# A weight fetched as eight long rows and turned by TensorE, with its cast moved from VectorE to ScalarE and GpSimd

## The chip, the cores and the metric

The kernel runs on one core of one Trainium2 chip. The metric is the device time of one execution in microseconds (us); the time before is the median of three runs, 203.02 us (202.86 to 203.06).

The names used below: PE is TensorE, DVE is VectorE, ACT is ScalarE, POOL is GpSimd, SP is SyncE. ACT and SP also issue DMAs (ACTq and SPq in the profile). A core has 16 DMA engines.

## The reference: what is computed

Two inputs `a` and `b` have the shape (8, 6400, 128), in float32. First a linear recurrence runs along the 6400 steps, for each of the 8 batches and 128 channels:

```python
h = a[:, t] * h + b[:, t]
out[:, t] = h
```

Its result, read as x with 51200 rows (tokens) of 128, goes through a mixture of eight small adapters. `logits = x @ w_gate` (w_gate is 128 x 8), the two largest logits of each token are taken, and a softmax over these two gives two weights. Each chosen expert e adds its weight times `(x @ A[e]) @ B[e]`, with A of shape (8, 128, 16) and B of shape (8, 16, 128). The result is x plus these two terms.

## The kernel before, in words

The 51200 tokens are cut into 100 chunks of 512 tokens. The chunks pass through these stages:

- SP loads `a` and `b` (line 295) into the tiles `a_tm` and `b_tm`, tokens on partitions: single chunks at both ends (256 KB for each of `a` and `b`), double chunks in the middle (512 KB).
- PE transposes both, by multiplying with an identity (line 310), so that channels are on partitions. ACT copies the turned `a` from PSUM to `a_st` (line 338); the turned `b` is read from PSUM.
- DVE runs the recurrence with a scan instruction, 512 steps at once, into `xT` in float16 (line 360).
- PE multiplies each block of 128 tokens with the 136 columns of `Awg_h` (line 434): 128 columns hold A for all experts, (e, r) in a row, and 8 hold the gate. ACT copies the result to `zl` (line 441).
- DVE, POOL and ACT make the gates of a group of chunks (lines 466 to 499), POOL or DVE multiplies them into `zl` (line 523), PE transposes the product (line 531), and ACT or DVE copies it (line 540).
- PE adds x and the product with `B_h` in PSUM (lines 558 and 559), ACT copies the sum to `outt` (line 566), and SP stores it (line 591).

The weights come at the start. Three DMAs on ACT's queue (line 261) fetch A, the gate and B into `cst_f`, in float32. A lies in memory as (e, d, r) and is wanted as d on partitions and (e, r) along them; the access pattern `moe_A.rearrange("e d r -> d e r")` does that in the DMA, in pieces of r = 16 floats, 64 bytes. One DVE cast (line 267) turns all 264 columns of `cst_f` into float16 in `cst_h`, of which `Awg_h` and `B_h` are parts. POOL makes the identity (lines 247 to 254), DVE casts it (line 263), and PE runs 14 transposes of the identity with itself (line 265), whose result is used by nothing, between the first real ones.

The order of the work is written out by hand. Each operation is added with its engine, a one-letter kind and the operations that it depends on; the strings in `ORDER` give the sequence of kinds on each engine, and within a kind the operations keep the order in which they were added. Each engine works strictly in its order. The wait of each operation is derived from its dependences (`waits`). PE's order begins with 11 transposes of kind "w" and then `ababwwwazb`: a and b of chunk 0, a and b of chunk 1, three more "w", a of chunk 2, the first logits matmuls "z" and b of chunk 2. ACT's order begins with the three weight DMAs, an activation that loads its table, three copies "a" and four copies "z". DVE's begins with the identity's cast, the weights' cast "c" and three scans. SP's order holds the loads x (of `a`) and y (of `b`) and the stores o. PSUM has eight banks; six of them rotate (`RING`) among the uses that name none, and each use waits until the bank's last content has been copied out.

A load waits until its slot of `a_tm` or `b_tm` has been transposed out (four slots of four blocks each for `a` and for `b`), an output copy until its part of `outt` has been stored (18 chunks fit).

Of the kernel before, what the change touches and what calls it, by code (L numbers as in the profile page):

```python
# [17 lines left out]
WARM = 14  # L18
# [3 lines left out]
RING = [0, 3, 4, 5, 6, 7]  # L22
ORDER = {
    "pe": (
        "wwwwwwwwwwwababwwwazbzzzaabzfzzffzzzfttffzdzdfzfzfzzzzfftfzzfddtffdzzzfdzzfzfztfzzfzztddfdfzfzdtfzzf"
        "dzzzzfttdffzddtfzzzfdddfzdzzffzttzzffzdtdzzffddzfztzffzzzddfdtffzzddfdztffzzzzdzftfztdfdzfddzdtzffzz"
        "dztzffdztdzdffzzzddtfztdzffdddztffzzdzzftdftzddzfdzfztzfzfddftzdzzfdtzzfzddtzzfddfftdzzfztfdzzztfddf"
        "fzzddtzdzfztfddfztzzffddfzztddtfzzzffdfzztdzddtffddztddfbtazddztzbzzbzzzadatdazbzzbdzztddtdztdddztdd"
        "dtddtddddttdd"
    ),  # L30
    "act": (
        "ccciaaazzzzaauzuazazazzzattaazzoozauazazzzzauatazzaootaauzzoaozzzaazztzaazztuzoaoaoazzoazzaozzzztaao"
        "auzooazzazoooazozazzaztuazzaozzoaaoozazztaazozzauootaazzoooazaazzzozzatzaauooazozooazzazzoazaouzzooa"
        "azzozouazoaazooozaazzzzotaaoozouzaozzatzzaoaoaozzzoazzazoouzazooaatozzzaauzozzoaoaaozzozzaotzaouozaz"
        "azaooazzootzazzuaaaozzzotooaauoozaooazoozzzzzzzaoauotauzzzozztoozouoozootooouuooooooo"
    ),
    "dve": (
        "icsss11223344s66ss1s2s31s2s43s64s6sss1s2s34s6ssss1s234ss6ssts1s23st4s6stss1s23s4sts6stss1s2s34ss1s62"
        "s3sts4s6s1s2t34s6stssts12st3s4ststs6sts1s234sts6ss1s234stssts612ts3s4sst6sstsst12346sssts1s234stss6s"
        "st12m34s6stststs1m2132436s4ss1m2m63m4t6mtm121m23m43m4t66tmmtt"  # L40
    ),
    "pool": (
        "cc8855pqpqrrmm585qp8rmmpqrmm85pqrmmmmm58mpqrmmmmmm58pqrmmmm8m5mpqrmmmm5m8mpqrmmmm8mm5qprm58mmmmmpqrm"
        "m58mmmpqrmmmmmm58pmqrm5mmmm8mqprmm5mm8qmprmmmm58mmmpqrmmmmm58mpqrmmm58mqmprmmm85mq8p5mrpq8r5pqr8558p"
        "pqqrr"
# [24 lines left out]
class Program:  # L70
# [8 lines left out]
    def add(self, eng, kind, deps, emit, sem=None, dur=0.0, lock=False, alt=None, size=0, ring=None):  # L79
        op = Op()  # L80
        op.i = len(self.ops)
        op.eng, op.kind, op.emit, op.sem = eng, kind, emit, sem
        op.deps = list({d.i: d for d in deps if d is not None}.values())
        op.cnt, op.clock, op.pos = 0, None, self.at
        op.dur, op.lock, op.alt, op.size = dur, lock or eng == "pool", alt, size
        op.ring = ring
        self.ops.append(op)
        return op
# [66 lines left out]
def bass_associative_scan_2x2__then__mixture_of_adapters_kernel(  # L155
# [9 lines left out]
    E = moe_w_gate.shape[1]  # L165
    R = moe_A.shape[2]
# [6 lines left out]
    of = out  # L173
# [16 lines left out]
    with ExitStack() as stack:  # L190
# [43 lines left out]
        eng = {}  # L234
# [19 lines left out]
        )  # L254
        o_c = []
        for key, dur, dst, src in (
            ("ca", 0.94, cst_f[:, 0:128].rearrange("p (e r) -> p e r", e=E), moe_A.rearrange("e d r -> d e r")),
# [9 lines left out]
        o_ch = P.add("dve", "c", o_c, lambda: eng["dve"].tensor_copy(cst_h[:, :], cst_f[:, :]), dur=0.3)  # L267
# [281 lines left out]
        def out_chunk(c, e_t):  # L549
# [15 lines left out]
            o_oe[c] = P.add("act", "o", [o_D[c]] + [out_user[p0 + k] for k in range(4)],  # L565
# [17 lines left out]
        def store(c, n):  # L583
# [5 lines left out]
            op = P.add(  # L589
                "sp", "o", [out_user[p0 + k] for k in range(nb)],  # L590
                lambda: eng["sp"].dma_start(
                    tokens(of, c, n, 4 * m), outt[:, p0 : p0 + nb, :].rearrange("p (h j) d -> p h (j d)", j=4 * m)),
                sem=dma_sem(f"st{p0 // 4}"), size=n if m > 1 else -n)
            for k in range(nb):
                out_user[p0 + k] = op
            o_st.append(op)
# [106 lines left out]
```

## Time and profile before

| | |
|---|---|
| median of three runs | 203.02 us (202.86 to 203.06) |
| the profiled execution | 202.82 us |
| its span, first to last instruction | 201.0 us |
| busy in the span: PE, DVE, ACT, POOL | 90%, 88%, 89%, 66% |
| HBM read and written | 52.56 MB and 26.21 MB, 392 GB/s over the span |

All numbers of the profile are from the one profiled execution. It was 0.2 us faster than the median, and 1.8 us of it lie outside the span. A row that begins with two times is a stretch of the span. "DMA share" is the time that the packets started in a stretch took, as a share of 16 engines' time: about 1 means full, and it can be a little over, since packets overlap. A row of DMA issues gives the tile and tensor, the queue, the count, the size of each and the median time from issue to the last byte's landing. In the chain of waits, a row is start, length and what was worked on. Rows of the timeline have start, length, engine, line, operation, tiles, shapes and the count of merged instructions, and in brackets the idle time before with what ended it.

### The profile page before, as it was taken

Reading aid. Unit: us, or ns where it says so; the run is one execution under the profiler, and the core shown is the slowest. Engines: PE = TensorE matmul, PEld = TensorE weight load, DVE = VectorE, ACT = ScalarE, POOL = GpSimd, SP = SyncE. Lnnn points to the kernel's source line nnn. Section 1 sums busy time; section 2 is a strip of 40 time slices with the busy share of each in tenths; the row PEclk is TensorE's granted clock in tenths of the full one; section 3 lists DMA queues with packets and bytes.
Section 4 is the critical chain, followed back from the end, with each engine's and each line's share of the span. In section 5 each row is a group of like instructions: output and inputs, shape, how many; then the busy total and the mean of one; then the engine's idle time right before and its main releaser. Section 6 shows DMA issues by size and latency. Waiting matters only on the chain.

```text
span 201.0 us, 7651 instructions
## 1 busy us (share of the span) xinstructions
PE 181.4 (90%) x3150; PEld 164.5 (82%) x3150; DVE 177.3 (88%) x265; ACT 178.4 (89%) x383; POOL 132.9 (66%) x209
## 2 busy tenths in 40 slices
PE   6878899899999996999999999999999998999840
PEld 6667678789989986999999999988888887998830
DVE  0799999999989996899999999998999999999830
ACT  3579899999999999699999999998899987999940
POOL 1061483959594954967898887697797978586400
PEclk9999999999999999799999999999999999999995
DMA  7999999999999999999999999999999999999992
GB/s 184 394 412 404 410 405 400 414 411 406 419 408 412 410 414 406 414 417 406 412 408 412 415 409 415 417 408 414 412 416 407 412 415 402 408 416 363 381 401 83
DMA packets 24690, 79.27 MB, mean 394 GB/s; under 512 B 3792, under 2 KB 3920, under 8 KB 24656
## 3 DMA queue, kind: packets, MB, share of 16 engines
q1 hardware_dynamic: 23328, 78.65, 98.0%
q8 instruction: 25, 0.41, 0.8%
q10 hardware_dynamic: 1328, 0.14, 0.5%
q14 instruction: 9, 0.07, 0.1%
HBM read 52.56 MB, written 26.21 MB: 392 GB/s over the span
## 4 chain that ended last, share of the span: by engine, by line
PE 36%; DMA 32%; ACT 17%; SPq 5%; DVE 4%; issue 2%; POOL 1%; ACTq 0%
DMA out_dram<-outt 16%; PE ps L310 14%; DMA a_tm<-in_a_dram 8%; DMA b_tm<-in_b_dram 7%; PE ps L558 6%; ACT outt L566 6%; PE ps L434 6%; SPq L295 5%; PE ps L559 5%; PE ps L531 5%; ACT zl L441 5%; ACT a_st L338 4%; DVE xT L360 2%; ACT zwT L540 2%; DVE zw L523 1%
## 5 line engine op out<-in xcount | busy, mean ns | idle before, releaser
L360 DVE TENSOR_TENSOR_SCAN xT<-a_st,xT,ps 128x512 f16<-128x512 f32 x96 | 120.3, 1253 | 7.6 <-PE ps L310 4.3
L523 POOL TENSOR_TENSOR zw<-zl,g 128x512 f16<-128x512 f32 x88 | 91.9, 1065 | 7.0 <-PE ps L531 5.4
L310 PE MATMUL ps<-ident_f,a_tm 64*128 64x64 f32 (+1 forms) x768 | 68.2, 231 | 6.5 <-DMA a_tm<-in_a_dram 2.7
L310 PE MATMUL ps<-ident_f,b_tm 64*128 64x64 f32 (+1 forms) x768 | 68.5, 231 | 1.2 <-DVE xT L360 1.0
L310 PEld LDWEIGHTS ps<-ident_f,a_tm 64*128 64x128 f32 (+1 forms) x768 | 56.2, 140 | 14.8 <-DMA a_tm<-in_a_dram 4.3
L338 ACT COPY a_st<-ps 128x512 f32<-128x512 f32 x100 | 61.5, 637 | 7.3 <-PE ps L310 7.0
L441 ACT COPY zl<-ps 128x408 f32<-128x408 f32 (+1 forms) x138 | 65.8, 540 | 0.9 <-PE ps L434 0.7
L566 ACT COPY outt<-ps 128x512 f32<-128x512 f32 x100 | 59.6, 640 | 3.7 <-PE ps L559 2.7
L558 PE MATMUL ps<-ident_h,xT 128*128 128x128 f16 x400 | 57.3, 232 | 0.7 <-issue 0.3
L310 PEld LDWEIGHTS ps<-ident_f,b_tm 64*128 64x128 f32 (+1 forms) x768 | 55.6, 139 | 2.2 <-DVE xT L360 1.1
L559 PE MATMUL ps<-cst_h,zwT 128*128 128x128 f16 x400 | 55.5, 221 | 0.0
L558 PEld LDWEIGHTS ps<-ident_h,xT 128*128 128x128 f16 x400 | 49.8, 142 | 2.8 <-ACT outt L566 0.4
L434 PE MATMUL ps<-cst_h,xT 128*128 128x136 f16 x400 | 42.3, 233 | 1.3 <-DVE xT L360 1.0
L559 PEld LDWEIGHTS ps<-cst_h,zwT 128*128 128x128 f16 x400 | 43.1, 108 | 0.2 <-issue 0.2
L434 PEld LDWEIGHTS ps<-cst_h,xT 128*128 128x128 f16 x400 | 32.2, 145 | 5.1 <-DVE xT L360 2.0
L531 PE MATMUL ps<-ident_h,zw 128*128 128x128 f16 x400 | 30.5, 219 | 0.9 <-DVE zw L523 0.6
L531 PEld LDWEIGHTS ps<-ident_h,zw 128*128 128x128 f16 x400 | 24.0, 98 | 2.0 <-DVE zw L523 1.0
L540 DVE COPY zwT<-ps 128x1024 f16<-128x1024 f16 (+1 forms) x32 | 21.0, 656 | 0.4 <-PE ps L531 0.2
L540 ACT COPY zwT<-ps 128x1024 f16<-128x1024 f16 (+1 forms) x20 | 20.6, 1037 | 0.3 <-PE ps L531 0.3
L480 POOL TENSOR_TENSOR dd<-m 128x24 f32<-128x24 f32 (+3 forms) x23 | 5.7, 249 | 19.2 <-DVE m L475 19.0
L497 POOL TENSOR_TENSOR g<-k,w 128x192 f32<-128x192 f32 (+3 forms) x23 | 11.0, 479 | 11.1 <-DVE k L482 7.8
L477 POOL TENSOR_TENSOR dd<-m 128x24 f32<-128x24 f32 (+3 forms) x23 | 5.9, 261 | 14.7 <-DVE m L475 14.7
(22 smaller groups left out, 86.4 us busy)
## 6 DMA issues: line engine op xcount, KB each, us to landing
a_tm<-in_a_dram SPq DMA_DIRECT2D x46, 512.0 KB, 15.3
b_tm<-in_b_dram SPq DMA_DIRECT2D x46, 512.0 KB, 15.2
out_dram<-outt SPq DMA_DIRECT2D x46, 512.0 KB, 14.9
a_tm<-in_a_dram SPq DMA_DIRECT2D x8, 256.0 KB, 8.4
b_tm<-in_b_dram SPq DMA_DIRECT2D x8, 256.0 KB, 8.6
out_dram<-outt SPq DMA_DIRECT2D x8, 256.0 KB, 8.6
cst_f<-in_moe_A_dram ACTq DMA_DIRECT2D x1, 64.0 KB, 3.4
cst_f<-in_moe_B_dram ACTq DMA_DIRECT2D x1, 64.0 KB, 4.3
```

The lines of the kernel that those rows point to most:

```text
L310: return [lambda k=k: eng["pe"].transpose(dv(k), src[r, k, :], ident_f[r, r]) for k in range(4 * m)]
L338: lambda: eng["act"].copy(a_st[:, ab, :], ps[:, ba.n, :]), dur=0.592)
L360: last = eng["dve"].tensor_tensor_scan(out=x_out[:, s0:s1], data0=a_in[:, s0:s1], data1=b_in[:, s0:s1], initial=init, op0=ALU.mult, op1=AL ...
L434: last = eng["pe"].matmul(ps[:, bk.n, k * W : k * W + W], xblock(b0 + k), Awg_h)
L441: lambda: eng["act"].copy(zl[:, z0 : z0 + n, :].rearrange("p k w -> p (k w)"), ps[:, bk.n, 0 : n * W]),
L497: lambda: eng["pool"].tensor_tensor(out=gg, in0=kk2, in1=bc(u2), op=ALU.mult), dur=pd)
L523: lambda me=me, wv=wv, zv=zv, gv=gv: eng[me].tensor_tensor(out=wv, in0=zv, in1=gv, op=ALU.mult),
L531: last = eng["pe"].transpose(ps[:, bt.n, :].bitcast(F16)[:, k * 128 : k * 128 + 128], zw[:, w + k // 4, k % 4, :], ident_h[:, :])
L540: f = (lambda: eng["act"].copy(dst, src())) if te == "act" else (lambda: eng["dve"].tensor_copy(dst, src()))
L558: eng["pe"].matmul(dst, xblock(b0 + k), ident_h[:, :], start=True, stop=False)
L559: last = eng["pe"].matmul(dst, zwT[:, w, k * 128 : k * 128 + 128], B_h, start=False, stop=True)
L566: lambda: eng["act"].copy(outt[:, p0 : p0 + 4, :].rearrange("p k d -> p (k d)"), ps[:, bo.n, :]), dur=0.6)
```

## The change

- A is fetched as it lies: eight rows, one for each expert, of 128 x 16 floats (8 KB), onto 8 partitions. They land in the first 16 blocks of `outt`, which are not yet used (`A_raw`).
- PE turns them: a new operation of kind "k", 16 transposes, one for each r, from [8, 128] (partition e, every 16th element) to columns r, 16 + r, ... of a PSUM bank. It stands in PE's order after b of chunk 1.
- The DVE cast "c" is gone. POOL casts the gate and B (136 columns), after making the identity. ACT copies A's 128 columns from PSUM to float16, in its order after the copy "a" of chunk 2.
- Of the 14 transposes "w" of the identity, 12 are left: 11 at the start and one between "k" and a of chunk 2.
- The output copies (line 566) name "k" as a further dependence.
- Stores can be cut by partitions (`SPLIT`); the table is empty, so that each store stays one DMA.

The diff's core:

```diff
-WARM = 14
+WARM = 12
+SPLIT = {}
 ORDER = {
     "pe": (
-        "wwwwwwwwwwwababwwwazbzzzaabzfzz...
+        "wwwwwwwwwwwababkwazbzzzaabzfzz...
     "act": (
-        "ccciaaazzzzaauzua...
+        "ccciaaakzzzzaauzua...
     "dve": (
-        "icsss11223344s66ss...
+        "isss11223344s66ss...
     "pool": (
-        "cc8855pqpqrrmm...
+        "ccc8855pqpqrrmm...
...
+        A_raw = outt[0:E, 0:R, :].rearrange("e k d -> e (k d)")
         o_c = []
         for key, dur, dst, src in (
-            ("ca", 0.94, cst_f[:, 0:128].rearrange("p (e r) -> p e r", e=E), moe_A.rearrange("e d r -> d e r")),
+            ("ca", 0.35, A_raw, moe_A.rearrange("e d r -> e (d r)")),
...
-        o_ch = P.add("dve", "c", o_c, lambda: eng["dve"].tensor_copy(cst_h[:, :], cst_f[:, :]), dur=0.3)
+        ak = Bank()
+
+        def turn_A():
+            for r in range(R):
+                last = eng["pe"].transpose(
+                    ps[:, ak.n, 0:128].rearrange("d (e r) -> d r e", r=R)[:, r, :],
+                    A_raw.rearrange("e (d r) -> e r d", r=R)[:, r, :], ident_f[0:E, 0:E])
+            return last
+
+        o_ak = P.add("pe", "k", [o_c[0], o_id], turn_A, dur=0.1 * R, ring=ak)
+        o_ch = [
+            P.add("pool", "c", o_c[1:], lambda: eng["pool"].tensor_copy(cst_h[:, 128:], cst_f[:, 128:]), dur=0.35),
+            P.add("act", "k", [o_ak], lambda: eng["act"].copy(cst_h[:, 0:128], ps[:, ak.n, 0:128]), dur=0.26),
+        ]
+        ak.evac = o_ch[1]
...
-            o_oe[c] = P.add("act", "o", [o_D[c]] + [out_user[p0 + k] for k in range(4)],
+            o_oe[c] = P.add("act", "o", [o_D[c], o_ak] + [out_user[p0 + k] for k in range(4)],
...
+            for i, hi in enumerate(SPLIT.get(c, []) + [128]):
+                parts.append(P.add(
+                    "sp", "p" if i else "o", deps,
+                    lambda lo=lo, hi=hi: eng["sp"].dma_start(
+                        tokens(of, c, n, 4 * m)[lo:hi],
+                        outt[lo:hi, p0 : p0 + nb, :].rearrange("p (h j) d -> p h (j d)", j=4 * m)),
```

45 lines of the change are left out of this document (23 added, 22 removed).

## The prediction

> **What bounds the kernel now.** I read the page's rows on DMA first, then the table by stretch of time, then the DMA issues at both ends of the span.
>
> ```profile
> q1 hardware_dynamic: 23328, 78.65, 98.0%
> q8 instruction: 25, 0.41, 0.8%
> q10 hardware_dynamic: 1328, 0.14, 0.5%
> q14 instruction: 9, 0.07, 0.1%
> ```
>
> The four queues fill the 16 DMA engines: 98.0 + 0.8 + 0.5 + 0.1 = 99.4% of the span. q1 holds the loads and stores that SP issues, q8 and q14 fetch instructions, and q10 is ACT's: it holds only the three weights. It moves 0.14 of 79 MB, yet has 1328 packets, and takes 0.5% of 201.0 us, 1.0 us on every engine. The table by stretch shows where the engines are full (columns: length, busy of the five engine rows, granted clock, DMA share, GB/s).
>
> ```profile
> 6.00:181.00 175.00, 165.88 (x2963) 150.87 (x2964) 166.23 (x234) 164.73 (x356) 126.29 (x186) 0.99 1.03 411
> 181.00:182.00 1.00, 1.00 (x18) 0.85 (x15) 1.00 (x5) 1.00 (x3) 0.00 (x0) 1.00 0.84 340
> ...
> 194.00:196.00 2.00, 0.00 (x0) 0.00 (x0) 0.00 (x0) 0.00 (x0) 0.00 (x0) 0.93 1.03 395
> 196.00:197.00 1.00, 0.00 (x0) 0.00 (x0) 0.00 (x0) 0.00 (x0) 0.00 (x0) 0.50 0.65 250
> ...
> 199.00:200.00 1.00, 0.00 (x0) 0.00 (x0) 0.00 (x0) 0.00 (x0) 0.00 (x0) 0.50 0.07 27
> ```
>
> From 6 to 181 us the share is 1.03, so there is always something queued. Only at 181 does it fall (0.84): some DMA engines have run dry and wait for stores that compute has not finished. After 194 us nothing computes, and the stores drain. They do not end together: the share is 0.65 from 196 us and 0.07 in the last full microsecond, and 0.07 of 16 engines is 1.1 engines; 27 GB/s is 1/15 of the 411 of a full stretch. So **one DMA engine works alone at the end**, about 3 us after most others are through, and the time is that of this engine. Was it ever idle? The issues at the two ends, which the view of DMA issues gives with their time to landing, answer that (the first row is of the first load, in an empty queue; the second of the last three stores, of the same size; the last is SP's closing wait):
>
> ```profile
> a_tm<-in_a_dram SPq DMA_DIRECT2D x1, 256.0 KB, 2.9
> ...
> out_dram<-outt SPq DMA_DIRECT2D x3, 256.0 KB, 6.5
> ...
> SPq L654 <- DMA out_dram<-outt: 5.9, 2, 5.5
> ```
>
> The last stores need 6.5 us to land, an empty queue 2.9: they stood 6.5 - 2.9 = 3.6 us behind earlier packets of the slowest engine. That engine was not waiting for compute even at the very end; the kernel's end has 3.6 us of room on the compute side. Earlier there is far more: the chain of waits holds a load, issued at 61.41 us, that took 16.71 us to land.
>
> ```profile
> 61.41 16.71 DMA a_tm<-in_a_dram
> ```
>
> So I take as the bound the sum of all packets on the slowest DMA engine, from about 2 us on. Whatever shortens this engine's list ends the kernel sooner by the same amount; whatever compute loses below 3.6 us costs nothing.
>
> **The change, part by part.**
>
> *A's transfer.* Now it goes out as (partition d) x (e) x 16 floats: 128 x 8 = 1024 pieces of 64 B, 64 on each engine. The queues in the stretch that holds their packets (2.82 to 3.66 us), a stretch of 0.20 us with one instruction packet of 8 KB, and one of 2.06 us with a packet of 16 KB:
>
> ```profile
> q10 hardware_dynamic: 1040, 0.07, 84.8%
> q1 hardware_dynamic: 91, 0.15, 48.2%
> ...
> q14 instruction: 1, 0.01, 9.7%
> ...
> q8 instruction: 1, 0.02, 3.2%
> ```
>
> 1040 packets (A's 1024 and 16 that end it) take 0.848 x 0.84 us = **0.71 us on each engine**. They go. In their place come 8 rows of 8 KB. No such row is in this trace; the 8 KB instruction packet is nearest, 0.097 x 0.20 x 16 = 0.31 us, and q1 agrees: 98.0% of 201.0 us x 16 engines for 78.65 MB is 40 ns per KB, 0.33 us for 8 KB. Eight rows cannot occupy 16 engines unless they are cut, so some engines get 0.31 us each and the others nothing. For the slowest engine the sum is between -0.71 + 0.31 = -0.40 us (a whole row falls on it) and -0.71 us. Part of a row may also be free, because the first microsecond of traffic is not full:
>
> ```profile
> 1.50:2.00 0.50, 0.48 (x3) 0.48 (x3) 0.23 (x1) 0.00 (x0) 0.00 (x0) 1.00 0.63 70
> 2.00:2.50 0.50, 0.50 (x4) 0.50 (x4) 0.00 (x0) 0.17 (x1) 0.00 (x0) 1.00 0.80 164
> ...
> 3.00:3.50 0.50, 0.50 (x5) 0.50 (x4) 0.00 (x0) 0.50 (x1) 0.00 (x0) 1.00 1.45 221
> ```
>
> Idle share there is 0.5 x (0.37 + 0.20) = 0.29 us per engine. Without 1024 descriptors ahead of them, the gate and B (the rest of q10, 1.0 - 0.7 = 0.3 us) come earlier too and could fall into it; that bounds the gain at all of q10, -1.0 us. I take **-0.65 us**, nearer to the end without a row, because either a row missing the slowest engine or half of it in the unfilled 0.29 us gives -0.55 to -0.71. Ends kept for the range: -0.40 and -1.0.
>
> [...] This trace shows one slow engine, but no number on it. [...]
>
> *SP's queue.* Nothing moves: the loads keep their order. SPLIT is empty, so each store stays one DMA. On ACT's queue the three issues remain, ahead of its first work.
>
> *PE.* Two of 14 warming transposes go, and kind "k", 16 transposes of [8, 128] to [128, 8], stands between chunk 1's b and chunk 2's a. Rows (timeline, and the chain for the first):
>
> ```profile
> 23.32 0.73 PE ps L310 x16
> ...
> 6.39 1.21 DVE L360 TENSOR_TENSOR_SCAN xT<-a_st,ps 128x512 f16<-128x512 f32 x1
> 6.56 0.66 PE L310 MATMUL ps<-ident_f,b_tm 128*128 128x128 f32 x4
> ...
> 7.05 0.49 PE L265 MATMUL ps<-ident_f 128*128 128x128 f32 x3
> ...
> 7.81 0.28 PE L434 MATMUL ps<-cst_h,xT 128*128 128x136 f16 x2
> 7.93 0.64 PE L310 MATMUL ps<-ident_f,b_tm 128*128 128x128 f32 x4
> 8.01 0.59 ACT L338 COPY a_st<-ps 128x512 f32<-128x512 f32 x1 [0.86 <-PE ps L310]
> ```
>
> Sixteen transposes of 64-row blocks take 0.73 us, of whole 128x128 blocks 16 x 0.66/4 = 2.64 us. Mine are smaller than the first, but stride over A; I take 1.2. Two warming ones less: 2 x 0.49/3 = -0.33. Net +0.9 us on PE (0.4 to 2.3).
>
> *The casts, a new wait.* Before, one DVE cast of all three weights stood ahead of the first scan:
>
> ```profile
> 6.18 0.30 DVE L267 CAST cst_h<-cst_f 128x264 f16<-128x264 f32 x1 [4.46 <-DMA cst_f<-in_moe_B_dram]
> ...
> 11.27 0.35 POOL L480 TENSOR_TENSOR dd<-m 128x4 f32<-128x4 f32 x2 [9.81 <-DVE m L475]
> ```
>
> The first scan (6.39) no longer stands behind it. GpSimd casts gate and B; it is idle to 11.27, so that is free, and if it took 1 us longer the first gating would still not see it. ACT casts A after chunk 2's evacuation, and PE's first logits matmul (7.81) now waits for that. By the old times: chunk 2's evacuation ends at 8.60, +0.9 for PE's extra work, +0.3 for the cast (DVE's cast of twice the columns took 0.30) is 9.8; less 0.65 for earlier loads, 9.15. That is 1.3 us late (0.8 to 2.7 with the ends above). Queued behind it on PE are chunk 2's b transposes (7.93), for which the third scan waits, and so all compute. **It stands beside the DMA backlog** and costs nothing at the end while below 3.6 us; without that cover it would cost its full 1.3 us.
>
> *The rest.* The output copies also wait for "k", long done at their first use. Instructions: PE has about 30 more in some 6300, so the 25 fetches on q8 should stay 25.
>
> **Sum:** -0.65 us on the slowest DMA engine, 0 elsewhere. The profiled execution took 202.82 us (1.8 outside its span of 201.0), so 202.2; the median is 203.02, and from there it is **202.4 us**. A measurement can tell about 0.2%, 0.41 us, from no change: faster means below 202.6.
>
> **Rivals.**
> 1. *A whole row lands on the slowest engine*, in full traffic: -0.40, 202.6 us, on the line between faster and same. For it: up to eight of sixteen engines carry one. Against: the 0.29 us of free share. [...]
> 2. *Nothing arrives at the end.* If the last engine idles somewhere in the early ramp, or loses time at each store in a way that gives the gain back: 203.0 us. For it: the share shows the mean of 16 engines, not the slowest. Against: 3.6 us of queue before the last store.
> 3. *The late start of compute reaches the end* (slower). Place: PE's wait for ACT's cast. The end is then the last store's issue plus 2.9 us; it decides once compute is more than 3.6 - 0.65 = 2.95 us late. The worst sum above is 2.7; with 1.5 us more, such as PE idling after A's landing, 4.2 us late gives 4.2 - 3.6 = +0.6, 203.6 us. For it: PE, DVE and ACT are busy 165 of 175 us, so nothing lost is made up by idle time. Against: the sum must nearly double.
> 4. *One more instruction packet on the slowest engine*, because code grows and moves: 0.032 x 2.06 x 16 = +1.05 us. With -0.40 that is 203.7. For it: the time hangs on a single engine's list. Against: 30 instructions are 0.5% of PE's.
>
> **How the numbers follow.** Forecast 0.45; rival 1 0.25; rival 2 0.12; rival 3 0.11; rival 4 0.07. The forecast counts 0.43 as faster and 0.02 as same; rival 1 is split in halves of 0.125. Faster: 0.43 + 0.12 = 0.55. Same: 0.02 + 0.13 + 0.12 = 0.27. Slower: 0.18. The range runs from all of q10 gone (203.02 - 1.0 = 202.0) through rivals 1 and 2 (203.0, and their 0.2 of spread: 203.2) and leaves out rivals 3 and 4. The forecast's own range is 202.0 to 202.55.
>
> **What would show it.** q10 should fall from 1328 packets to about 310 and from 0.5% to about 0.2%. In the table by stretch, 3.0 to 3.5 us should move near 390 GB/s instead of 221. The first scan should start before 6.39, the first logits matmul after 7.81. The last full microsecond should still show one engine's share, the last stores some 6 us to landing (less if compute is late: at 2.9 rival 3 holds). I am wrong if the share at the end shows no lone engine, if q8 or q14 count more packets, or if the last store is issued after about 197 us.

## The result and the profile after

The changed kernel is **slower**: 204.96 us median (203.35 to 206.68, 7 runs), the kernel before 203.03 us (202.86 to 203.16, 7 runs); the ratio is 1.0072, 95% interval 1.0054 to 1.0091. The forecast was 202.4 us and a range up to 203.2. The profiled execution took 204.56 us (span 202.8), 1.74 us more than that of before. Ratios here leave out disturbed runs; medians hold all.

The queues of the changed kernel (packets, MB, share of 16 engines' span):

```profile
q1 hardware_dynamic: 23328, 78.65, 98.1%
q8 instruction: 25, 0.41, 0.8%
q10 hardware_dynamic: 304, 0.14, 0.3%
q14 instruction: 9, 0.07, 0.1%
```

The pieces are gone (1328 packets are 304), and q8 and q14 are as before: rival 4 is out. But q10 keeps 0.3%, for 1024 packets fewer. The table by stretch of time (the last three columns are granted clock, DMA share, GB/s):

```profile
2.00:2.50 0.50, 0.50 (x4) 0.50 (x4) 0.00 (x0) 0.28 (x1) 0.00 (x0) 1.00 0.41 66
2.50:3.00 0.50, 0.50 (x4) 0.50 (x3) 0.00 (x0) 0.50 (x1) 0.00 (x0) 1.00 0.89 348
3.00:3.50 0.50, 0.50 (x4) 0.50 (x3) 0.00 (x0) 0.50 (x1) 0.00 (x0) 1.00 1.28 193
3.50:4.00 0.50, 0.50 (x3) 0.23 (x2) 0.00 (x0) 0.21 (x2) 0.00 (x0) 1.00 0.91 168
6.00:181.00 175.00, 166.59 (x2931) 151.67 (x2930) 162.13 (x228) 161.73 (x350) 123.61 (x180) 1.00 1.03 407
...
196.00:197.00 1.00, 0.97 (x15) 0.68 (x12) 0.28 (x1) 0.57 (x1) 0.00 (x0) 1.00 1.01 399
...
201.00:202.00 1.00, 0.00 (x0) 0.00 (x0) 0.00 (x0) 0.00 (x0) 0.00 (x0) 0.50 0.10 39
```

The stretch from 3.0 to 3.5 us, which was to rise from 221 to near 390 GB/s, fell to 193, and the next one from 383 to 168, with a share of 1.28 and 0.91: the engines are occupied and move half the bytes. And the middle moves 407 GB/s where it was 411. Compute now works at 196 us, when it had ended by 194 before. At the end one engine or two still work alone (0.10 of 16). The start of compute, from the timeline (start us, duration, engine, line, operation, and idle time before it):

```profile
4.93 1.11 PE L329 MATMUL ps<-ident_f,a_tm 128*128 128x128 f32 x4 [0.80 <-DMA a_tm<-in_a_dram]
...
6.77 0.30 POOL L283 CAST cst_h<-cst_f 128x136 f16<-128x136 f32 x1 [5.30 <-DMA cst_f<-in_moe_B_dram]
6.94 1.22 DVE L379 TENSOR_TENSOR_SCAN xT<-a_st,ps 128x512 f16<-128x512 f32 x1 [5.21 <-PE ps L329]
...
8.54 1.93 PE L276 MATMUL ps<-ident_f,outt 8*128 8x8 f32 x16
...
10.67 1.06 PE L329 MATMUL ps<-ident_f,a_tm 128*128 128x128 f32 x4
...
11.76 0.59 ACT L357 COPY a_st<-ps 128x512 f32<-128x512 f32 x1 [3.39 <-PE ps L329]
12.25 0.27 ACT L284 CAST cst_h<-ps 128x128 f16<-128x128 f32 x1
...
12.62 0.39 PE L453 MATMUL ps<-cst_h,xT 128*128 128x136 f16 x2 [0.89 <-issue]
...
13.90 1.28 DVE L379 TENSOR_TENSOR_SCAN xT<-a_st,xT,ps 128x512 f16<-128x512 f32 x1 [3.97 <-PE ps L329]
```

Read it as a sum of small losses: chunk 0 waits for its load to 4.93 us (before, its transposes began at 3.92); four transposes take 1.06 us where four took 0.66; the sixteen of A take 1.93; ACT's cast stands behind chunk 2's evacuation; the first logits start at 12.62 instead of 7.81 us, **4.8 us late** where 1.3 were forecast. SP feels it, in its waits (total, times, longest) of before, then of after:

```profile
SPq L591 <- ACT outt L566: 39.8, 23, 5.7
```

```profile
SPq L614 <- ACT outt L585: 50.2, 23, 7.5
...
SPq L679 <- DMA out_dram<-outt: 4.0, 2, 3.7
```

SP issues stores and loads in one order; while a store waits for its output, the loads behind it aren't issued. These waits grew by 10.4 us, and the last stores had 3.7 us of queue to drain instead of 5.5. The chain of work that ended last, on the two pages, before and after:

```profile
PE 36%; DMA 32%; ACT 17%; SPq 5%; DVE 4%; issue 2%; POOL 1%; ACTq 0%
```

```profile
PE 65%; DVE 15%; ACT 11%; issue 4%; DMA 2%; POOL 1%; DVEq 0%
```

Before, a third of the chain is DMA; after, its only DMA is the wait for the first load, and from there on it runs through compute to the last output copies. These end at 197.60 us (196.43 + 1.17), before at 193.99 (192.82 + 1.17), 3.6 us earlier. The bytes tell where the DMA engines came short, above all in the first 11 us and from 40 to 66 us; the stretch from 181 to 196 us is the third. For before, then for after:

```profile
1.00:12.00 11.00, 9.18 (x69) 7.86 (x70) 5.78 (x14) 5.77 (x13) 0.94 (x5) 1.00 0.99 336
...
40.00:66.00 26.00, 25.65 (x483) 23.54 (x482) 25.09 (x34) 25.92 (x58) 18.79 (x27) 1.00 1.03 411
...
181.00:196.00 15.00, 11.37 (x172) 10.04 (x169) 10.81 (x31) 11.60 (x25) 5.87 (x17) 0.99 0.96 381
```

```profile
1.00:12.00 11.00, 9.40 (x48) 8.14 (x48) 2.73 (x3) 2.89 (x5) 0.59 (x2) 1.00 0.93 318
...
40.00:66.00 26.00, 24.77 (x450) 22.21 (x449) 23.79 (x31) 25.04 (x54) 21.09 (x27) 1.00 1.02 392
...
181.00:196.00 15.00, 13.99 (x209) 12.57 (x208) 13.97 (x36) 14.03 (x32) 8.98 (x25) 1.00 0.90 360
```

Bytes short, at 411 GB/s: (336 - 318) x 11 / 411 = **0.5 us at the start**, where a gain was forecast, and (411 - 392) x 26 / 411 = **1.2 us from 40 to 66 us**. From 181 to 196 us another (381 - 360) x 15 / 411 = 0.8 us is short, and some 0.5 us in the stretches between; in return the drain behind 196 us has about 1.0 us less of idle engines. So the first two, together 1.7, come near the 1.74 by which the execution is longer only because the rest nearly cancels. What happens from 40 to 66 us is in SP's timeline of after and in the DMA view of 58 to 60 us (its slices of 0.05 us):

```profile
54.35 5.01 SPq L614 DMA_DIRECT2D out_dram<-outt  x2
59.40 1.20 SPq L314 DMA_DIRECT2D b_tm<-in_b_dram  x2
```

```profile
DMA  9999996639699389929301952690599295299198
...
DMA packets 164, 0.59 MB, mean 295 GB/s; under 512 B 20, under 2 KB 20, under 8 KB 164
```

For 5 us SP issues two stores and no load, and at its end the queues run dry. The two losses call for two theories, named C and D in the expectations below.

### The profile page after: what moved, and what is told of

It is laid out like the page before. It is cut to its first block, busy times and chain, and to the rows that moved or that the text cites. A ratio compares the mean times of both kernels' runs of the same rounds, so it can differ in the third digit from the quotient of the medians.

```text
span 202.8 us, 7680 instructions
## 1 busy us (share of the span) xinstructions
PE 185.2 (91%) x3164; PEld 168.2 (83%) x3164; DVE 176.6 (87%) x264; ACT 178.4 (88%) x384; POOL 133.3 (66%) x210
## 4 chain that ended last, share of the span: by engine, by line
PE 65%; DVE 15%; ACT 11%; issue 4%; DMA 2%; POOL 1%; DVEq 0%
PE ps L329 26%; PE ps L453 12%; DVE xT L379 10%; PE ps L577 10%; PE ps L550 8%; PE ps L578 7%; ACT outt L585 3%; ACT a_st L357 3%; ACT zl L460 3%; DMA a_tm<-in_a_dram 2%; DVE zw L542 2%; ACT zwT L559 1%; PE ps L276 1%; DVE zwT L559 1%; DVE L L490 0%
## 5 line engine op out<-in xcount | busy, mean ns | idle before, releaser
L329 PE MATMUL ps<-ident_f,a_tm 64*128 64x64 f32 (+1 forms) x768 | 70.0, 234 | 3.9 <-issue 2.1
L329 PE MATMUL ps<-ident_f,b_tm 64*128 64x64 f32 (+1 forms) x768 | 69.7, 232 | 1.5 <-DVE xT L379 0.9
L460 ACT COPY zl<-ps 128x408 f32<-128x408 f32 (+1 forms) x138 | 66.5, 547 | 2.2 <-PE ps L453 2.0
L329 PEld LDWEIGHTS ps<-ident_f,a_tm 64*128 64x128 f32 (+1 forms) x768 | 57.3, 141 | 11.9 <-issue 4.6
L329 PEld LDWEIGHTS ps<-ident_f,b_tm 64*128 64x128 f32 (+1 forms) x768 | 56.7, 140 | 2.2 <-issue 1.1
L577 PE MATMUL ps<-ident_h,xT 128*128 128x128 f16 x400 | 56.3, 230 | 0.1
L578 PE MATMUL ps<-cst_h,zwT 128*128 128x128 f16 x400 | 54.5, 219 | 0.0
L577 PEld LDWEIGHTS ps<-ident_h,xT 128*128 128x128 f16 x400 | 49.3, 141 | 2.3 <-ACT zwT L559 0.3
L453 PE MATMUL ps<-cst_h,xT 128*128 128x136 f16 x400 | 42.9, 235 | 3.3 <-DVE xT L379 2.0
```

The lines of the kernel that those rows point to most:

```text
L329: return [lambda k=k: eng["pe"].transpose(dv(k), src[r, k, :], ident_f[r, r]) for k in range(4 * m)]
L453: last = eng["pe"].matmul(ps[:, bk.n, k * W : k * W + W], xblock(b0 + k), Awg_h)
L460: lambda: eng["act"].copy(zl[:, z0 : z0 + n, :].rearrange("p k w -> p (k w)"), ps[:, bk.n, 0 : n * W]),
L577: eng["pe"].matmul(dst, xblock(b0 + k), ident_h[:, :], start=True, stop=False)
L578: last = eng["pe"].matmul(dst, zwT[:, w, k * 128 : k * 128 + 128], B_h, start=False, stop=True)
```

## The experiments

**Theory C**: the late start of compute costs, through SP's loads, which come late. **Theory D**: the eight rows cost the DMA engines more than the 1024 pieces did. Each kernel ran beside the kernel before on the same chip. The table gives the median (runs), the ratio with its interval, the start of the first logits matmul in the profile, and the GB/s of the two stretches:

| kernel | us (runs) | ratio [95%] | first logits | 1-12 us | 40-66 us |
|---|---|---|---|---|---|
| before | 203.0 | 1 | 7.81 | 336 | 411 |
| after | 204.96 (7) | 1.0072 [1.0054, 1.0091] | 12.62 | 318 | 392 |
| again | 203.9 (12) | 1.0054 [1.0032, 1.0077] | 11.80 | 324 | 394 |
| late5 | 203.14 (10) | 1.0014 [1.0002, 1.0025] | 11.01 | 342 | 406 |
| late7 | 205.56 (4) | 1.0093 [1.0070, 1.0116] | 13.08 | 337 | 378 |
| small33 | 203.15 (8) | 0.9999 [0.9986, 1.0013] | 10.26 | 332 | 407 |
| cast_split | 203.01 (10) | 1.0004 [0.9995, 1.0013] | 8.83 | 340 | 411 |
| warm_more | 203.67 (6) | 1.0034 [1.0022, 1.0047] | 11.16 | 323 | 410 |
| k_early | 203.28 (10) | 1.0019 [1.0007, 1.0031] | 10.45 | 329 | 411 |
| rows_last | 205.55 (4) | 1.0124 [1.0057, 1.0190] | 11.01 | 331 | 391 |
| rows_last_k | 203.29 (11) | 1.0016 [1.0007, 1.0024] | 10.02 | 331 | 411 |
| rows_last_kw | 203.26 (11) | 1.0016 [1.0007, 1.0025] | 9.65 | 332 | 411 |
| rows_too | 204.18 (4) | 1.0059 [1.0046, 1.0072] | 10.34 | 315 | 411 |
| no_A | 202.35 (7) | 0.9974 [0.9963, 0.9985] | 8.04 | 348 | 411 |
| rows8 | 203.73 (10) | 1.0028 [1.0017, 1.0038] | 8.64 | 327 | 411 |
| rows64 | 202.99 (11) | 0.9994 [0.9984, 1.0003] | 7.80 | 347 | 411 |
| rows8x8 | 203.29 (11) | 1.0015 [1.0006, 1.0025] | 9.50 | 321 | 411 |
| spread8 | 203.08 (11) | 1.0012 [1.0003, 1.0020] | 8.56 | 339 | 411 |
| half_k | 202.92 (12) | 0.9998 [0.9989, 1.0006] | 8.69 | 328 | 412 |
| quarter_k | 202.62 (11) | 0.9983 [0.9974, 0.9992] | 9.83 | 337 | 411 |

The last two columns part the causes: the first is below 335 only where 64 KB came in rows of 4 or 8 KB or into eight partitions (small33 is the exception: in its profile nothing moved from 1.5 to 2.0 us, where before had 70 GB/s), the second is below 410 only where compute starts late, though not everywhere it does (warm_more).

### The changed kernel again (again)

No edit.

> The changed kernel once more, unchanged. Theory C (compute starts late: TensorE runs at half clock until a point that differs from run to run, about 16.4 us in the first profile): single times spread over 203.3 to 206.7 us again, and in this profile the first logits matmul starts later than 7.81 us by an amount that goes with the time; 9 to 10 us would go with about 203.5, 12 to 13 us with about 204.6. Theory D (the eight rows load the DMA engines, compute is a bystander): times spread too, but first logits matmul and time are unrelated, and the first load lands at about 4.9 us each time.

First logits 4.0 us late, 394 GB/s from 40 to 66 us. Chunk 0 waits for its load to 4.87 us again, as theory D says, and 11.80 us goes with a profiled execution of 204.09 us, as theory C says. The loss is there again, and its size varies from run to run: eleven of the twelve runs took 203.34 to 205.80 us, where those of the kernel before beside them lie within 0.7 us (202.57 to 203.24).

### Late compute without any other transfer (late5, late7, small33)

late5 and late7, the kernel before with 30 and 49 more warming transposes between chunk 1 and chunk 2; small33 puts 32 transposes of 8 rows there instead of two of the three:

```diff
-        "wwwwwwwwwwwababwwwazbzzzaabzf...
+        "wwwwwwwwwwwabab" + "w" * 33 + "azbzzzaabzf...     late5; late7: 52
+        "wwwwwwwwwwwababkkwazbzzzaabzf...                  small33; k = 16 transposes of ident_f[0:8, :]
...
```

> The kernel before with 30 more transposes of the identity (nothing reads them) between chunk 1 and chunk 2: at 0.16 us each TensorE comes to chunk 2 about 4.9 us later at full clock, and no DMA is changed. Theory C: the late start alone empties the DMA queues at 40 to 66 us and at the end, 204.3 to 205.3 us. Theory D: 203.0 us, since the DMA work is the same and the prediction's 3.6 us of room were far too small a count.

> The kernel before with 49 more transposes of the identity between chunk 1 and chunk 2 (30 of them made the first logits matmul start at 11.0 us and left the time at 203.1): at about 0.12 us each the first logits matmul comes at about 13.2 us, later than in the changed kernel (11.8 and 12.6), with no DMA changed. Theory C (late compute empties the DMA queues around 60 us): 204.0 to 205.5 us, spread over more than 0.5 us, and load rows issued between 46 and 60 us land within 9 us instead of 11 to 13. Theory D (the rows' price on the DMA engines is the whole loss): 203.0 to 203.3 us.

> The kernel before with 32 transposes of 8 rows by 128 of the identity in place of two of the three warming transposes between chunk 1 and chunk 2, nothing else: no other transfer, no other wait, no cast. It tells whether the small transposes themselves bring TensorE to half speed. If they do, they take about 3.8 us (0.12 us each, as the sixteen of the changed kernel) and the chunk transposes after them take 1.06 us per four instead of 0.66, first logits 3.5 to 4.5 us later than before, 203.2 to 203.8 us; if the clock there is held and only the waits let it fall, they take 1.2 to 2 us, the ones after them 0.60 to 0.66 us per four, and the time is 203.0 us.

late5's transposes took 3.77 us, so that the first logits were only 3.2 us late: nearly all of it is covered (0.28 us remain), and theory C's 204.3 us or more did not come. late7 was 5.3 us late and lost 1.9 us (ratio 1.0093), with the DMA of the first 11 us untouched. From the table by stretch of late7:

```profile
1.00:12.00 11.00, 10.19 (x74) 9.43 (x75) 2.93 (x4) 2.66 (x4) 0.29 (x1) 1.00 0.96 337
...
40.00:66.00 26.00, 23.45 (x408) 20.69 (x407) 22.13 (x28) 22.77 (x49) 20.54 (x26) 0.94 1.01 378
...
181.00:196.00 15.00, 14.19 (x208) 13.16 (x207) 14.48 (x39) 14.53 (x34) 8.84 (x21) 1.00 0.75 298
```

337 GB/s at the start, as before, and 378 instead of 411 from 40 to 66 us, lower than in the changed kernel. (The clock of 0.94 comes from 62 us on, behind 2 us without any work for TensorE.) This is theory C alone, and **it is shown** that compute which only starts late costs time, and that in these two kernels the cover runs out between 3.2 and 5.3 us. It costs in both places: 2.1 us of bytes are missing from 40 to 66 us, and 3.0 us from 181 to 196 us, (381 - 298) x 15 / 411, of which the drain makes good a part. The last store was issued at 201.35 us (179.77 + 21.58 in SP's timeline), and the span ended 2.95 us later, at 204.3: near the 2.9 us that the prediction names for an empty queue.

small33 looks at a side question, the clock. From its timeline and its table by stretch:

```profile
7.33 2.13 PE L268 MATMUL ps<-ident_f 8*128 8x8 f32 x32
...
9.56 0.90 PE L312 MATMUL ps<-ident_f,a_tm 128*128 128x128 f32 x4
...
10.48 1.06 PE L312 MATMUL ps<-ident_f,b_tm 128*128 128x128 f32 x4
```

```profile
10.00:13.00 3.00, 3.00 (x19) 2.55 (x17) 1.42 (x4) 1.84 (x5) 0.00 (x0) 0.50 1.03 413
```

32 small transposes take 2.13 us, 0.067 us each; those of A in the changed kernel take 1.93 / 16 = 0.12 us each. The expectation tied the half clock to their length, and that was wrong: they were short, and chunk 2's transposes behind them still took 0.90 and 1.06 us per four, with TensorE never idle and a granted clock of 0.50 from 10 to 13 us. The same is seen in four more profiles, again, warm_more, rows_last and rows_last_k: full speed (0.60 to 0.66 us per four) ahead of the small transposes or just behind them, and 1.06 us per four within 2 us of their end. late5, with 33 whole transposes in their place, stayed at 0.60, and so did cast_split with 0.92 us of idle time. So it goes with the small transposes, though not always: in rows_last_kw they came at half speed (1.06 and 1.12 us per four ahead of them) and full speed followed (0.60). With the first logits 2.5 us late, the time stayed that of before.

### The casts alone (cast_split)

The kernel before, with the casts on GpSimd and ACT and with A still fetched as 64 B pieces:

```diff
-        o_ch = P.add("dve", "c", o_c, lambda: eng["dve"].tensor_copy(cst_h[:, :], cst_f[:, :]), dur=0.3)
+        o_ch = [
+            P.add("pool", "c", o_c[1:], lambda: eng["pool"].tensor_copy(cst_h[:, 128:], cst_f[:, 128:]), dur=0.35),
+            P.add("act", "k", o_c[:1], lambda: eng["act"].copy(cst_h[:, 0:128], cst_f[:, 0:128]), dur=0.26),
+        ]
...
```

> The kernel before with its old fetch of A and all 14 warming transposes, but the casts as in the changed kernel: GpSimd casts gate and B, ScalarE casts A after its copy for chunk 2, no transposes of A. First scan earlier than 6.39 us, first logits matmul at 8.6 to 9.2 instead of 7.81. Theory C: 1 us is covered, 202.9 to 203.2 us. Theory D: the same. A time over 203.6 would say that the wait for ScalarE's cast is itself the cause, against both.

203.01 us, ratio 1.0004: nothing. The first scan is earlier (5.67 us), the first logits 1.0 us later, covered. The prediction's zero for this part holds.

### The start of compute in the changed kernel (warm_more, k_early, rows_last)

warm_more has 19 warming transposes ahead of chunk 0; k_early turns A ahead of chunk 0 and casts it ahead of all evacuations; rows_last issues the eight rows behind gate and B:

```diff
-        "wwwwwwwwwwwababkwazbzzzaab...
+        "wwwwwwwwwwwwwwwwwwwababkwazbzzzaab...     warm_more
+        "wwwwwwwwwwwkababwazbzzzaab...             k_early; act: "ccciaaak" is "cccikaaa"
-            ("ca", 0.35, A_raw, moe_A.rearrange("e d r -> e (d r)")),
             ("cw", 0.16, cst_f[:, 128:W], moe_w_gate[:, :]),
             ("cb", 0.16, cst_f[:, W : W + 128], moe_B.rearrange("e r d -> (e r) d")),
+            ("ca", 0.35, A_raw, moe_A.rearrange("e d r -> e (d r)")),     rows_last; act: "ccicaaak"
...
```

> The changed kernel with 20 instead of 12 identity transposes, 19 of them at the start, so that TensorE does not fall idle before the first load lands at 4.9 us; DMAs as in the changed kernel. Theory C+D (rows cost about 0.5 us on the slowest engine, the rest is compute that starts late because TensorE stays at half clock): chunk transposes at 0.60 to 0.66 us per four instead of 1.06, first logits matmul at 9.5 to 11, time 203.3 to 203.7 us with a spread under 0.5 us. Theory C alone: 202.3 to 202.8 us. Theory D alone: no change, 203.9 to 205.

> The changed kernel with the 16 transposes of A put ahead of chunk 0 on TensorE, into the time in which it waits for the first load, and ScalarE's cast of A ahead of its copies; DMAs as in the changed kernel. Theory C+D: the first logits matmul no longer waits for A, it starts at 9 to 10.5 us; 203.3 to 203.7 us. Theory C alone: 202.3 to 202.8. Theory D alone: as the changed kernel, 203.9 or more.

> The changed kernel with the eight rows issued last on ScalarE's queue, after the table load (about 3.7 us instead of 0.74), so that they come into a running stream and not ahead of the first load. Theory C+D: the first load lands at 3.3 us or sooner, TensorE does not fall to half clock, the engines without a row gain 0.5 us over before and those with one lose nothing; 202.5 to 203.1 us. If the rows cost the same in a full stream as at the start (0.6 us on the slowest engine), 203.4 us or more.

warm_more and k_early bring back the 40 to 66 us stretch (410 and 411 GB/s) and come down to 203.67 and 203.28 us, the two ends of what theories C and D together expected (203.3 to 203.7), but not to the time of before: 323 and 329 GB/s remain at the start. rows_last was to be the fastest and was the slowest of the three, with the start of the loads mended: its transposes ran at half speed (granted clock 0.90 from 1 to 12 us and 0.86 from 12 to 40, against 1.00 in both for before), and 391 GB/s were left from 40 to 66 us. Its first logits came at 11.01 us, as in late5, and it lost 2.5 us where late5 lost 0.28; but its granted clock stayed at 0.50 from 10 to 20 us, and late5's at 1.00. So the start of the first logits alone doesn't tell how late compute is, and the cover has no single length in it. (The column of the clock misses some of this: in the changed kernel it says 1.00 while four transposes take 1.06 us.)

### A turned between chunk 0 and chunk 1 (rows_last_k, rows_last_kw)

rows_last, with "k" moved ahead on TensorE and ACT; kw with four more warming transposes:

```diff
-        pe "wwwwwwwwwwwababkwazbzzzaab...     act "ccicaaakzzzz...
+        pe "wwwwwwwwwwwabkabwazbzzzaab...     act "ccicakaazzzz...     rows_last_k
+        pe "wwwwwwwwwwwabkwwabwwazbzzzaab...                           rows_last_kw
...
```

> The changed kernel with the eight rows issued behind gate and B and, on TensorE, the sixteen transposes of A between chunk 0 and chunk 1, ACT's cast of A right behind chunk 0's evacuation: first logits no longer wait for a cast that stands behind chunk 2. Theory C (the late start of compute is what costs): first logits at 9.0 to 10.5 us, DMA queues no longer empty at 50 to 60 us, 202.6 to 203.3 us, same as the kernel before or a little faster. Theory D alone (the rows cost more than the pieces whatever compute does): 203.3 to 203.6 us.

> As the kernel with the rows last and A turned between chunk 0 and chunk 1, with four more warming transposes, two on either side of chunk 1's, to keep TensorE at work while it waits. If the half clock after the sixteen transposes comes from TensorE waiting, the chunk transposes behind them go at 0.60 to 0.66 us per four and the time is 202.6 to 203.1 us; if it comes from the small transposes themselves, they go at 1.06 us per four, the first logits are 0.3 to 0.6 us later than in that kernel, and the time is the same as that kernel's or 0.2 us above it.

Both 1.0016, 0.3 us above before, with 411 GB/s in the middle: the loss of theory C is gone. 203.29 us stands on the border between the two ranges expected (up to 203.3, and from there on), so that the time decides nothing; that something is left is said by the ratio (1.0007 to 1.0024) and the 331 GB/s. In kw the chunk transposes behind A's ran at full speed (0.60 us per four), in k at 0.91 to 1.06; the first logits came 0.4 us apart, and the time was the same: full speed, as for waiting, and no gain, as for the small transposes, so that the expectation of kw is met in neither form.

### What the rows cost (rows_too, no_A, rows8)

rows_too fetches the eight rows besides A's pieces; no_A leaves A's fetch out; rows8 is no_A with the eight rows, read by nothing:

```diff
+        o_raw = P.add("act", "c", [], lambda: eng["act"].dma_start(A_raw, moe_A.rearrange("e d r -> e (d r)")), ...)   rows_too, rows8
...
-            ("ca", 0.94, cst_f[:, 0:128].rearrange("p (e r) -> p e r", e=E), moe_A.rearrange("e d r -> d e r")),     no_A, rows8
+        o_c = [P.add("pool", "c", [], lambda: eng["pool"].memset(cst_f[:, 0:128], 0.0), dur=0.3)]                    no_A, rows8
...
```

> The kernel before, which also fetches A as eight rows of 8 KB into the unused part of outt, ahead of the three weight DMAs; nothing reads the rows. Theory D: the first load lands at about 4.9 instead of 3.6 us, eight DMA engines run 0.65 us behind from then on, and the time is 203.4 to 203.9 us. Theory C: the rows matter only as far as they keep TensorE waiting for the first load: first logits matmul about 1.3 us later than 7.81, time within 0.4 us of 203.0, unless TensorE falls to half clock, and then over 203.5.

> The kernel before without A's fetch: GpSimd sets A's columns of the weights to zero, so the result lacks the terms with A; nothing takes the place of the 1024 pieces of 64 B. The theory of the prediction (0.71 us of every engine's list goes with the pieces): about 202.3 us, 0.7 us under the kernel before. Theory D (the pieces fill time in which the engines have little else, so that little comes back; the rows, put ahead of the first loads, cost more than that): 202.7 to 203.0 us. Theory C says nothing on it, since compute starts no later than before.

> The kernel without A's fetch, with the eight rows of 8 KB fetched first on ACT's queue into eight partitions, as in the changed kernel; nothing reads them, so neither TensorE nor a cast waits for them, and the result lacks the terms with A. Against the kernel without A's fetch (202.35 us) it prices the rows alone. The prediction's price (0.31 us on eight engines, nothing on the others): at most 0.3 us more, 202.4 to 202.7 us. Theory D (about 0.37 us on eight engines, and a stretch of half a microsecond or more after the rows in which all engines are busy but move half the bytes): 0.8 to 1.1 us more, 203.1 to 203.4 us.

rows_too: 204.18 us, 1.2 us above before, more than theory D expected (203.4 to 203.9), with 411 GB/s in the middle although the first logits were 2.5 us late. no_A: the pieces' removal gains 0.0026 x 203.0 = **0.53 us** (0.3 to 0.75); the forecast's 0.71 is inside, and D's guess that little comes back is wrong. rows8: 1.0028 - 0.9974 = 0.0054, so the rows **cost 1.1 us** (0.65 to 1.5 from the ends of the two intervals). The median, 203.73 us, is above what theory D expected, and 1 us above what the prediction's price gives. That the rows cost more than the pieces is said directly by rows8's ratio to the kernel before, 1.0028 (1.0017 to 1.0038). q10 of no_A, then of rows8, with their tables by stretch:

```profile
q10 hardware_dynamic: 288, 0.07, 0.2%
```

```profile
1.00:12.00 11.00, 9.95 (x76) 9.38 (x78) 6.11 (x14) 5.89 (x14) 1.24 (x7) 1.00 0.93 348
```

```profile
q10 hardware_dynamic: 304, 0.14, 0.4%
```

```profile
1.00:12.00 11.00, 9.77 (x64) 8.43 (x64) 5.22 (x14) 5.56 (x11) 0.61 (x4) 1.00 0.94 327
...
40.00:66.00 26.00, 25.25 (x474) 23.01 (x473) 25.07 (x35) 25.91 (x56) 18.78 (x27) 1.00 1.03 411
```

The eight rows add 0.2% of the span, 0.4 us on the mean of 16 engines, 0.8 us if all of it falls on eight of them; and over all engines (348 - 327) x 11 / 411 = 0.56 us of bytes are missing. How the 1.1 us divide between the two wasn't measured.

### Why the rows cost so much (rows64, rows8x8, spread8)

As rows8, with the same 64 KB cut in other ways:

```diff
-  outt[0:E, 0:R, :].rearrange("e k d -> e (k d)")                                    <- "e d r -> e (d r)"                  rows8
+  outt[0:64, 0:2, :].rearrange("p k d -> p (k d)")                                   <- "e (a x) r -> (e a) (x r)", a=8     rows64
+  outt[0:E, 0:32, :].rearrange("e (a b) d -> e a (b d)", b=4)[:, :, 0:256]           <- "e (a x) r -> e a (x r)", a=8       rows8x8
+  outt[0:29:4, 0:R, :].rearrange("e k d -> e (k d)")                                 <- "e d r -> e (d r)"                  spread8
```

> The same with the same 64 KB fetched as 64 rows of 1 KB into 64 partitions. If it is the length of the rows, or that so few partitions and engines take all of the 64 KB, that makes the rows dear, the stretch of half the bytes is gone and the time is 202.4 to 202.6 us (64 KB are 0.16 us of 411 GB/s); if any further fetch ahead of the first loads costs as much, it is 203.0 us or more.

> The same with the 64 KB fetched as 64 pieces of 1 KB, eight into each of eight partitions. If the length of a row is what costs, this goes as the 64 rows in 64 partitions, 202.4 to 202.6 us; if it is that all 64 KB go into eight partitions, it goes as the eight rows of 8 KB, 203.1 to 203.4 us, with the stretch of half the bytes in its table of windows.

> The kernel without A's fetch, with the eight rows of 8 KB fetched first on ACT's queue into partitions 0, 4, 8 to 28 instead of 0 to 7, and read by nothing: the same eight rows, the same length, only other partitions. [...] If it is the eight rows on eight engines: 203.1 to 203.7 us, as with the rows in partitions 0 to 7.

The table by stretch of rows64:

```profile
1.00:12.00 11.00, 8.96 (x70) 7.83 (x70) 5.83 (x14) 5.85 (x13) 1.10 (x6) 1.00 0.95 347
```

347 GB/s: in this execution, one of the shortest (202.45 us), 64 rows of 1 KB into 64 partitions cost the DMA next to nothing. The median, 202.99 us, isn't as low as was expected: the runs fall into two groups, 202.44 to 202.76 and 202.99 to 203.16, and why stays open. Pieces of the same 1 KB into eight partitions give 321 GB/s and 1.0015: the length of a row isn't the main cause. Eight rows of 8 KB into partitions 0, 4 to 28 instead of 0 to 7 give 339 GB/s and 1.0012; 203.08 us is at the edge of the 203.1 to 203.7 expected if eight rows on eight engines are the cause, and below rows8's 203.73: only spreading the rows over other partitions brings back 12 of the 347 - 327 = 20 GB/s, and by the ratios 0.16 of the 0.34% between rows8 and rows64 (0.3 of 0.7 us, with intervals nearly as wide). What is left wasn't taken apart further. It can be the number of engines: beside no_A's 288 packets q10 has 80 more in rows64, 72 in rows8x8, and 16 in rows8 and spread8, which is the pieces and 16 packets that end them in the first, 8 in the others. A's pieces had 16, as many as there are engines. If each engine used has one of these, which no view here shows, rows64 used sixteen engines and the other three eight. Why other partitions make the rows cheaper isn't shown either.

### The change made to pay (half_k, quarter_k)

rows_last_k, with A as 16 rows of 4 KB or 32 rows of 2 KB, turned into as many columns, and cast by two or four ACT copies that put the parts in their partitions (quarter_k):

```diff
-        A_raw = outt[0:E, 0:R, :].rearrange("e k d -> e (k d)")
+        A_raw = outt[0 : 32, 0 : 4, :].rearrange("e k d -> e (k d)")
-            ("ca", 0.35, A_raw, moe_A.rearrange("e d r -> e (d r)")),
+            ("ca", 0.35, A_raw, moe_A.rearrange("e (h d) r -> (e h) (d r)", h=4)),
-                    ps[:, ak.n, 0:128].rearrange("d (e r) -> d r e", r=R)[:, r, :],
-                    A_raw.rearrange("e (d r) -> e r d", r=R)[:, r, :], ident_f[0:E, 0:E])
+                    ps[0:32, ak.n, 32 * r : 32 * r + 32],
+                    A_raw.rearrange("e (d r) -> e r d", r=R)[:, r, :], ident_f[0:32, 0:32])
...
+            v = ps[0:32, ak.n, 0:512].rearrange("d (r e h) -> d h e r", r=R, h=4)
+            for h in range(4):
+                last = eng["act"].copy(cst_h[32 * h : 32 * (h + 1), 0:128].rearrange("d (e r) -> d e r", r=R), v[:, h])
```

> A working version for the theory that few partitions make the rows dear: the changed kernel with A fetched last on ACT's queue as 16 rows of 4 KB into 16 partitions (one for each expert and half of A's rows), turned by 16 transposes of [16, 64] between chunk 0 and chunk 1, and cast by two ACT copies, one for each half. If partitions and engines decide: the table by stretch moves 335 to 345 GB/s between 1 and 12 us (332 with eight rows), 202.7 to 203.1 us. If eight rows of 8 KB or sixteen of 4 KB make no difference: 203.3 us, as the kernel with eight rows fetched last.

> The same with 32 rows of 2 KB into 32 partitions, 16 transposes of [32, 32] and four ACT copies. If partitions decide: 342 to 347 GB/s between 1 and 12 us and 202.5 to 202.9 us, unless the four copies (some 0.9 us on ACT) start compute more than 3 us late, when 40 to 66 us would move less than 410 GB/s and the time be 203.0 us or more. If the number of partitions makes no difference: 203.3 us.

quarter_k takes 202.62 us, ratio 0.9983 (0.9974 to 0.9992): **0.35 us faster than the kernel before**, at 337 GB/s at the start, less than expected, and 411 in the middle. half_k is the same as before; its 328 GB/s are of its longest execution. Its transposes, and those of quarter_k, from their timelines:

```profile
6.21 1.08 PE L276 MATMUL ps<-ident_f,outt 16*64 16x16 f32 x16 [0.36 <-DMA outt<-in_moe_A_dram]
```

```profile
6.04 1.03 PE L276 MATMUL ps<-ident_f,outt 32*32 32x32 f32 x16 [0.20 <-DMA outt<-in_moe_A_dram]
```

Sixteen take 1.08 and 1.03 us, not 1.93: they have fewer columns, and their results lie side by side in PSUM rather than 16 words apart. small33's have all 128 columns, lie side by side, and take 0.067 us each, as these do; that points to the 16 words. No kernel changes these alone.

## Why the prediction was wrong, step by step

- **The bound, one DMA engine's list of packets.** It held as long as compute was in time. Taking the pieces off the list gave 0.53 us for the 0.71 forecast, and putting rows on it (rows_too) cost 1.2 us with no other change to the program. In the changed kernel it held no longer by itself: the chain that ended last has 2% of DMA instead of 32%.
- **The term "-0.65 us" for A's transfer.** Wrong, in the part that priced the rows: "some engines get 0.31 us each and the others nothing". The 0.31 came from an instruction packet of 8 KB in other surroundings. The rows cost 1.1 us: q10 alone has some 0.8 us if they lie on eight engines, and behind them all engines move fewer bytes (168 to 193 GB/s in the changed kernel, 277 to 324 in rows8 from 3.0 to 5.5 us). The first rival allowed -0.40; the sum is -0.53 + 1.1 = +0.6.
- **"Part of a row may also be free, because the first microsecond of traffic is not full."** Wrong: the rows stand ahead of the first loads, and chunk 0's transposes wait for theirs to 4.93 us instead of 3.92. In rows_last_k and kw, with the rows behind gate and B, they start at 3.93 and 3.92.
- **"1.3 us late (0.8 to 2.7)".** Wrong, the mis-sized term of the sum: 4.8 us. The pieces: 1.0 us because the load landed later, counted as 0.65 earlier; A's sixteen transposes 1.93 instead of 1.2 us; chunk transposes 1.06 instead of 0.66 us per four, which no step reckoned with. The runs show a slow start that ends at another point each time: in no_A chunk 0 and 1 ran at 1.06 and 0.96 us per four and chunk 2 at 0.60 from 7.60 us on, in rows64 chunk 0 and 1 at 0.85 and 0.60 to 0.66, and eleven runs of again lie 2.5 us apart. In the changed kernel four transposes still took 1.06 us at 12.80 us, though from 4.93 us on TensorE was never idle for more than 0.9 us; what ends the slow start isn't shown.
- **"Costs nothing at the end while below 3.6 us", "earlier there is far more".** The first half came out near the truth: 3.2 us late cost 0.28, 5.3 us late 1.9, where 5.3 - 3.6 is 1.7. The second half was the error of method: the 16.71 us to landing at 61.41 us was read as room. It is how far SP is ahead of the slowest engine, and SP's lead is made of buffers that compute has freed; late compute takes the lead away, loads are issued late, and the other engines run dry. The times to landing of a store issued from 46 to 54 us, before and after, fit that:

```profile
out_dram<-outt SPq DMA_DIRECT2D x1, 512.0 KB, 13.5
```

```profile
out_dram<-outt SPq DMA_DIRECT2D x1, 512.0 KB, 5.4
```

- **Rival 3** had the right mechanism, the point (about 3 us) nearly right, and a price of 0.6 us (203.6) for what comes to some 0.9 below. Its place, the last store, is seen in late7, which ends 2.95 us behind the last issue; in the changed kernel the last store was issued 3.6 us later than before (198.0 and 194.4 us) and the span ended 4.8 instead of 6.6 us behind it, so that 1.8 us were lost. It said nothing of the loads that come late from 40 to 66 us. It got 0.11 since its worst sum was 2.7 us. If rows and late compute simply add up, 1.0072 is 1.0028 for the rows (rows8) and some 0.0044, 0.9 us, for compute.
- **The casts, instruction fetches**: nil, as forecast (cast_split; q8 and q14). SP's order didn't change either, but what it issues came late.
- **The signs named.** Wrong were the 390 GB/s, the first scan before 6.39 us (6.94) and q10's 0.2%; right were q10's packets and the first logits after 7.81. The last sign of error also came: SP's chain of stores ended at 186.22 + 11.78 = 198.0 us, past 197:

```profile
186.22 11.78 SPq L614 DMA_DIRECT2D out_dram<-outt  x11
```

Open stays which engine is the slowest, whether it carried a row, and how the loss of the changed kernel divides between that engine, which works nearly alone from 200 us on, and the late compute.

## What to carry to other kernels

Count a transfer's cost by where it lands as well as by its packets: 64 KB into eight neighbouring partitions cost 1.1 us here, into 64 partitions some 0.4 (0 to 0.8 from the ends of the intervals), and the same change pays (0.35 us) once its rows are 32 in 32 partitions, last in the queue, with the work on them ahead of what waits for it. A long time from issue to landing isn't room for late compute: room is how late the work that frees buffers can be before loads are issued late, and doubling that lateness with harmless work (late5, late7) measures it. And read bytes moved, not the share of busy time, for what a DMA stretch is worth: the share stood at 1.02 where 5% of the bytes were missing.

## What the runs showed of the hardware

- A DMA share of 0.9 to 1.3 stood beside 168 to 193 GB/s in the half microseconds behind the eight rows, and 0.99 beside 295 GB/s where a queue ran dry and filled again.
- no_A had TensorE at half speed until 7.3 us (0.96 to 1.06 us for four transposes, 0.60 from 7.60 us on) and was the fastest kernel of all (202.35 us; it leaves A out), with the first logits 0.2 us late: no cost of the half speed is seen there.
- Sixteen small transposes of A took 1.93, 1.92 and 1.93 us in after, warm_more and rows_last_kw, whether the transposes ahead of them ran at half (1.06 us per four in after, 1.12 in rows_last_kw) or at full speed (0.66 in warm_more).
